# Decay tables by running products in two layouts, first-chunk scores from raw r*k, one rotation for raw weights, and a new order of work

## The chip, the cores and the metric

The kernel runs on 1 core of one Trainium2 chip. The metric is the device time of the whole kernel in microseconds (us). A change of 0.2% of the time before is 1.74 us.

## The reference

Three layers in a row, all in fp32. B = 4 batches, H = 8 heads, S = 768 steps, D = 48; 3072 tokens, d_model 384, d_ff 2048.

```
for t in range(S):                                   # attention with a decaying state
    cur = einsum('bhd,bhe->bhde', u * k[t], v[t])
    y[t] = einsum('bhd,bhde->bhe', r[t], state + cur)
    state = w * state + einsum('bhd,bhe->bhde', k[t], v[t])
x = y as (3072, 384)
h = x @ w_in;  x = (maximum(h, 0) + alpha * minimum(h, 0)) @ w_out      # FF1
h = x @ w_in2; out = (h * tanh(softplus(h))) @ w_out2                    # FF2
```

w (8 x 48) lies between 0.85 and 0.95.

## The kernel before

**Attention by chunks.** A chunk is 128 steps. Inside it the loop becomes matrices: r is multiplied by powers of w that rise with t and k by powers that fall (table RK, by `prep_rk`, L374), and `scores` (L451) multiplies the two on TensorE for all pairs of steps. `masked` (L455, VectorE) copies the strict triangle of the scores into a tile A whose diagonal was preset with c = sum of r*u*k (`preset_first`, L432 on GpSimd or L430 on ScalarE). For the first chunk c comes from `c_first`: a product m of r and k (L389, VectorE), times uw by 8 small matmuls (L393), copied by ScalarE (L395). Since m is made of tiles that `prep_rk` has already scaled by w to the powers t and -(t+1), uw is u*w. `attend0` (L466) multiplies A by v, and `x_first` (ScalarE L160) and `x_first_lo` (VectorE L163) split the result into a high and a low part, fp32r each. The first chunk is units 0 to 3, one per batch. `states_first` (L532) makes the state after it, and ScalarE copies it into T (L534).

Later chunks are units 4 to 23, half a chunk of two batches each. Their heads lie in another layout, the "seats", and `prep_pair` (L380, VectorE) scales r and k by the middle of RKs, the table RK in that layout. Four transfers, SBUF to SBUF, make RKs from RK (`load_RKs`, L271), and `tables_seat` (GpSimd) takes the decay of a half chunk, w64, from it.

**Tables.** `tables` (L308 to L325) makes powers of w by doubling in 24 or so small VectorE instructions, and RK by two multiplies of 112x512.

**FF1.** A slot is 128 of the 2048 features for 512 tokens (units 0 to 3 are one such block): `mA_h` (9 matmuls of 128x512, L238: high x high, high x low, low x high for three pieces of d_model), `mA_g` (ScalarE relu L605, VectorE L607, gives g), `mA_hi` (ScalarE L160), `mA_lo` (VectorE L163), `mA_out` (9 matmuls, L637). In `mA_h` the first matmul needs the high parts of x and of the weight, the second the low part of x, the third the low part of the weight.

**Weights.** Each of the 16 slices of FF1's weights comes raw by one transfer of 768 KB (`more_raw`, `load_raw`, L180), is scaled in two ScalarE passes (`w_scale`, L186 and L187), put together on VectorE (`w_join`, L192) and split (`w_hi` L160 or GpSimd, `w_lo` L163). Slices 0 to 3 land in the places of the later weights w4 to w7, slices 7 to 10 in w9, w11, w13, w15, all others in three buffers "wraw" in rotation: a load there waits for the join of the slice that held the buffer.

**Order.** All work is written out in a plan and sorted by a number per step: the table PLACES gives it by the step's name (a step without an entry has a default), and entries that begin with "?" move a step to another engine. Each engine runs its instructions in that order. `keep_warm` steps (L590) are filler matmuls on a tile of zeros: 8 at the front and 10 in the plan.

Of the kernel before, what the change touches and what calls it, by code (L numbers as in the profile page):

```python
# [54 lines left out]
def more_state(u):  # L55
# [5 lines left out]
    "dma_start": -133.1356, "load_unit 0": -123.5208, "dma_start#": -121.3588, "load_unit 1": -120.2047,  # L61
    "tables": -119.5105, "load_k 0": -116.8818, "load_unit 2": -116.4952, "load_k 2": -116.4633,
    "keep_warm 3########": -115.8159, "dma_start##": -115.6181, "prep_rk 0": -115.3668, "more_raw 1": -115.0907,
    "load_k 1": -114.4474, "load_unit 3": -114.0374, "more_raw 3": -113.632, "pad_v 1": -113.2894,
    "load_unit 4": -111.9708, "more_raw 2": -111.7638, "load_k 3": -111.37, "<lambda> 0": -109.0738,
    "load_unit 5": -107.6626, "tables_u": -106.0724, "<lambda> 1": -105.5347, "memset": -105.2417,
    "keep_warm 3######": -105.0553, "c_first 0": -104.9975, "tensor_scalar": -104.9222, "load_RKs": -104.605,
    "pad_v 0": -103.892, "<lambda> 2": -103.757, "prep_rk 1": -103.5598, "preset_first 0": -103.0121,
    "<lambda> 3": -102.9784, "more_raw 7": -102.3381, "keep_warm 3###": -101.6704, "prep_rk 2": -101.4031,
    "w_scale (0,0)": -101.3169, "keep_warm 3": -101.1634, "keep_warm 3#########": -100.8119, "scale_Kn": -100.7696,  # L70
# [982 lines left out]
```

## Time and profile before

| | |
|---|---|
| median of 3 runs | 872.24 us (871.73 to 872.92) |
| profiled execution, its own time | 871.41 us |
| its span | 869.7 us |
| TensorE (PE) busy, share of the span | 861.4 us, 99% |
| PE weight loads (PEld) | 712.4 us, 82% |
| VectorE (DVE) | 630.6 us, 73% |
| ScalarE (ACT) | 617.5 us, 71% |
| GpSimd (POOL) | 98.9 us, 11% |
| granted TensorE clock | 1.00 |

PE's busy time includes fillers. A share over the whole span says little about the first 51 us, where attention's head, the first weights and the first slots run together; there the rows must be read one by one.

### The profile page before, as it was taken

What the parts mean: (1) busy time and instruction counts of PE and PEld (TensorE: products, weight loads), DVE (VectorE), ACT (ScalarE), POOL (GpSimd) and SP (SyncE); (2) the same over time, 40 slices, a digit from 0 to 9 for tenths busy, and PEclk for the clock granted to TensorE, in tenths of its full rate; (3) what the DMA queues carried; (4) which work ended last, traced back from release to release, by engine and by line L of the source; (5) the groups of instructions that cost most, each with busy time, mean ns of one, the idle gap of its engine ahead of it and who ended that gap; (6) DMA issues with size and microseconds to landing.
All of it is one profiled execution on the core that took longest, in us unless ns stands there. A gap on an engine that the chain in (4) does not pass through costs nothing.

```text
span 869.7 us, 16740 instructions
## 1 busy us (share of the span) xinstructions
PE 861.4 (99%) x6380; PEld 712.4 (82%) x6380; DVE 630.6 (73%) x1021; ACT 617.5 (71%) x1198; POOL 98.9 (11%) x119
## 2 busy tenths in 40 slices
PE   9899999999999999999999999999999999999998
PEld 5778878888888888888888888888888888888897
DVE  6789756657656565554666887887887887887876
ACT  3787765454445545444555998998998998998886
POOL 3624322111122111100002000000000000000000
PEclk9999999999999999999999999999999999999999
DMA  9986365255344426211620200110110110100101
GB/s 316 273 230 208 108 190 146 78 176 152 135 134 141 141 87 212 73 56 64 211 82 35 109 1 1 26 48 1 26 48 1 26 49 0 26 12 1 26 12 37
DMA packets 65840, 80.41 MB, mean 92 GB/s; under 512 B 39712, under 2 KB 52960, under 8 KB 65760
## 3 DMA queue, kind: packets, MB, share of 16 engines
q1 hardware_dynamic: 65200, 79.24, 30.4%
q8 instruction: 50, 0.82, 0.4%
q14 instruction: 30, 0.25, 0.1%
q10 hardware_dynamic: 560, 0.10, 0.1%
HBM read 61.16 MB, written 15.73 MB: 88 GB/s over the span
## 4 chain that ended last, share of the span: by engine, by line
PE 97%; ACT 2%; DVE 1%; issue 0%; POOL 0%; DVEq 0%; POOLq 0%
PE h L238 44%; PE acc L637 22%; PE sc L758 8%; PE acc L758 8%; PE yt L758 4%; PE acc L756 3%; PE acc L590 2%; PE sc L451 2%; PE sc L756 1%; PE h L482 1%; PE yt L503 1%; PE sc L496 1%; PE yt L482 1%; ACT Ah L422 1%; PE h L466 0%
## 5 line engine op out<-in xcount | busy, mean ns | idle before, releaser
L238 PE MATMUL h<-x,w 128*128 128x512 f32 x1728 | 415.8, 390 | 2.8 <-ACT w L160 1.6
L238 PEld LDWEIGHTS h<-x,w 128*128 128x128 f32 x1728 | 323.8, 188 | 72.3 <-ACT w L160 2.0
L637 PE MATMUL acc<-ghi,w 128*128 128x512 f32 x516 | 174.9, 394 | 0.0
L605 ACT ACTIVATE m<-h 128x512 f32<-128x512 f32 x96 | 57.2, 596 | 89.7 <-PE h L238 89.6
L637 PEld LDWEIGHTS acc<-ghi,w 128*128 128x128 f32 x516 | 96.8, 188 | 21.3
L607 DVE SCALAR_TENSOR_TENSOR g<-m,oma,h 128x512 f32<-128x512 f32 x96 | 71.6, 746 | 56.9 <-ACT m L605 55.9
L160 ACT ACTIVATE ghi<-g 128x512 fp32r<-128x512 f32 x86 | 54.1, 629 | 70.9 <-PE acc L637 42.7
L163 DVE TENSOR_TENSOR glo<-g,ghi 128x512 fp32r<-128x512 f32 x86 | 60.3, 701 | 56.3 <-ACT ghi L160 56.1
L637 PE MATMUL acc<-glo,w 128*128 128x512 f32 x258 | 100.4, 389 | 0.0
L695 DVE SCALAR_TENSOR_TENSOR a<-ghi,h 128x512 f32<-128x512 f32 x96 | 66.1, 688 | 37.8 <-ACT ghi L692 31.3
L695 DVE SCALAR_TENSOR_TENSOR g<-s,c 128x512 f32<-128x512 f32 x95 | 66.7, 702 | 22.7 <-ACT s L692 20.6
L703 ACT ACTIVATE m<-h 128x512 f32<-128x512 f32 x96 | 56.4, 588 | 35.0 <-PE h L238 35.0
L163 DVE TENSOR_TENSOR gloB<-g,ghiB 128x512 fp32r<-128x512 f32 x105 | 72.1, 686 | 6.8 <-ACT ghiB L160 6.8
L692 ACT ACTIVATE ghi<-m,biases 128x512 f32<-128x512 f32 x96 | 69.6, 725 | 3.2
L160 ACT ACTIVATE ghiB<-g 128x512 fp32r<-128x512 f32 x105 | 64.8, 617 | 8.8 <-PE acc L637 6.9
L692 ACT ACTIVATE glo<-ghi,biases 128x512 f32<-128x512 f32 x96 | 68.1, 710 | 0.1
L692 ACT ACTIVATE s<-glo,biases 128x512 f32<-128x512 f32 x96 | 68.1, 709 | 0.0
L692 ACT ACTIVATE s<-s,biases 128x512 f32<-128x512 f32 x96 | 68.0, 708 | 0.0
L758 PE MATMUL sc<-ghiB,w 128*128 128x512 f32 x192 | 66.9, 389 | 0.0
L695 DVE SCALAR_TENSOR_TENSOR b<-ghi,a 128x512 f32<-128x512 f32 x96 | 65.7, 684 | 0.1
L695 DVE SCALAR_TENSOR_TENSOR c<-glo,b 128x512 f32<-128x512 f32 x95 | 65.7, 692 | 0.0
L758 PE MATMUL acc<-ghiB,w 128*128 128x512 f32 x192 | 61.7, 389 | 0.0
(198 smaller groups left out, 1157.7 us busy)
## 6 DMA issues: line engine op xcount, KB each, us to landing
wrawr<-in_w SPq DMA_DIRECT2D x24, 768.0 KB, 5.2
nat<-in_nat SPq DMA_DIRECT2D x40, 288.0 KB, 4.3
w2d<-wj SPq DMA_DIRECT2D x16, 384.0 KB, 2.6
wraw<-w2d SPq DMA_DIRECT2D x16, 384.0 KB, 3.0
rk<-in_rkT SPq DMA_DIRECT2D x40, 128.0 KB, 3.0
x2d<-xo SPq DMA_DIRECT2D x6, 768.0 KB, 3.5
x<-x2d SPq DMA_DIRECT2D x6, 768.0 KB, 4.6
rk<-in_rkT SPq DMA_DIRECT2D x40, 96.0 KB, 2.8
```

The costliest lines, as they stand in the source:

```text
L160: act.activation(out=hi, in_=src, func=AF.Copy)
L163: eng.tensor_tensor(out=lo, in0=src, in1=hi.bitcast(F32), op=ALU.subtract)
L238: pe.matmul(h, w_in(layer, f, a, c), x[:, b, c, :], start=(k == 0), stop=(k == 3 * KC - 1))
L451: pe.matmul(sc_t[u][h][HALF[i], o], rk[ROWS[h], 1, j, s], rk[ROWS[h], 0, j, t], start=True, stop=True)
L605: act.activation(out=m, in_=hA[s], func=AF.Relu, scale=-1.0)
L607: dve.scalar_tensor_tensor(out=g, in0=m, scalar=oma[:, f:f + 1], in1=hA.pop(s), op0=ALU.mult, op1=ALU.add)
L637: pe.matmul(acc[0][c], w_out(0, f, a)[:, c * 128:(c + 1) * 128], g[b], start=(f == 0 and k == 0), stop=(f == NF - 1 and k == 2))
L692: act.activation(out=out, in_=in_, func=AF.Square, scale=scale, bias=fin[bias])
L695: dve.scalar_tensor_tensor(out=out, in0=in0, scalar=scalar, in1=in1, op0=op0, op1=ALU.mult)
L703: act.activation(out=bnew("t", n), in_=v["h", n], func=AF.Tanh, scale=0.5)
L756: pe.matmul(acc[1][t][:, :DM], g[a][:, t * C:(t + 1) * C], w_out(1, f, b), **se)
L758: pe.matmul(acc[1][t], w_out(1, f, a)[:, t * 128:(t + 1) * 128], g[b], **se)
```

## The change

- `tables` makes the powers by running products (`tensor_tensor_scan` on VectorE, 68 and 20 elements), one reciprocal of 88 elements, and fills RK by four multiplies of 112x256.
- The seats' table RKs (half as long now, 64 steps) is no longer copied by transfers. Four small transfers on ScalarE's queue bring w in the seats' layout (`wts`), `powers_seat` repeats the running products on VectorE, and `tables_seat` fills RKs by four multiplies of 112x128 on GpSimd ("?seat": 1) and copies w64.
- `m_first` takes the product of raw r and k, ahead of `prep_rk`; the small matmuls then use u itself (`ut`), and `tables_u` goes. The products lie in the buffers glo, glo, ghi and g, where all four shared g.
- Slices 7 to 10 of the raw weights lose their own places and go through the three wraw buffers.
- PLACES is rewritten as a whole. Step switches: presets of the diagonal on ScalarE for unit 3 (before: 2), decay of T on ScalarE for units 4, 6, 8 (before: 8), the sum of unit 7 on ScalarE (before: 9, 10), low parts of the weights 2, 4, 13 on GpSimd (before: 2, 13, 14), fillers 5 and 7 in small pieces (before: 5).

```diff
 PLACES = {
-    "dma_start": -133.1356, "load_unit 0": -123.5208, ...
+    "tables": -134.74003, "powers_seat": -134.4197, "dma_start": -128.3432, "load_unit 0": -125.2362, ...
...
     wt = att.tile([PR, NPR], F32, name="wt")
     w64 = att.tile([PR, NPR], F32, name="w64")
-    uw = att.tile([PR, NPR, 2], F32, name="uw")
-    w96 = att.tile([PR, 40], F32, name="w96")[:, 0:NPR]
+    ut = att.tile([PR, NPR, 2], F32, name="ut")
+    small = att.tile([PR, 40], F32, name="w96")
+    w96, wts = small[:, 0:NPR], small[:, 8:8 + NPR]
...
+    def rows(x):
+        return x.rearrange("d (p n) -> d p n", p=NPR)
+
+    def powers(part, w):
+
+        n, m = NPR * 17, NPR * 5
+        step, first, power, inverse = (part[:, o:o + n + m] for o in (0, 96, 192, 288))
+        P, A = rows(power[:, 0:n]), rows(power[:, n:])
+        iP, iA = rows(inverse[:, 0:n])[:, :, 1:17], rows(inverse[:, n:])
+
+        def scan(at):
+            dve.tensor_tensor_scan(out=power[:, at], data0=step[:, at], data1=first[:, at], initial=0.0, op0=ALU.mult,
+                                   op1=ALU.add)
+
+        pool.memset(part, 0.0)
+        for x in (rows(first[:, 0:n]), rows(first[:, n:])):
+            pool.memset(x[:, :, 0], 1.0)
+        dve.tensor_copy(rows(step[:, 0:n])[:, :, 1:17], w.unsqueeze(2).to_broadcast([PR, NPR, 16]))
+        scan(slice(0, n))
+        dve.tensor_copy(rows(step[:, n:])[:, :, 1:5], P[:, :, 16:17].to_broadcast([PR, NPR, 4]))
+        scan(slice(n, n + m))
+        dve.reciprocal(out=inverse, in_=power)
+        return ((P[:, :, 0:16], iA, A), (iP, A, iA))
+
+    def fill(eng, table, parts, n):
+
+        for i, (p, less, more) in enumerate(parts):
+            o = table[:, i].rearrange("d p (a b) -> d p a b", b=16)
+            for a, g in ((0, less[:, :, n:0:-1]), (n, more[:, :, 0:n])):
+                eng.tensor_tensor(out=o[:, :, a:a + n], in0=g.unsqueeze(3).to_broadcast([PR, NPR, n, 16]),
+                                  in1=p.unsqueeze(2).to_broadcast([PR, NPR, n, 16]), op=ALU.mult)
+
     def tables():
 
-        part = new("g")[0:PR].rearrange("d (p x) -> d p x", p=NPR)
-        P, iP, G, iG = part[:, :, 0:17], part[:, :, 32:48], part[:, :, 64:73], part[:, :, 80:89]
-        sq = part[:, :, 96:98].transpose([0, 2, 1])
-
...
+        fill(dve, RK, parts, 4)
+        A = parts[0][2]
+        dve.tensor_tensor(out=w96, in0=A[:, :, 4], in1=A[:, :, 2], op=ALU.mult)
+
+    seat_t = {}
+
+    def powers_seat():
+        seat_t[0] = powers(per.tile([128, 512], F32, tag="w0", name="seat")[0:PR], wts)
 
     def tables_seat():
 
-        pool.tensor_tensor(out=w64, in0=RKs[:, 1, :, 0], in1=RKs[:, 0, :, HC + 1], op=ALU.mult)
-
-    def load_RKs():
-        by_seat(RKs, RK, slice(None))
+        fill(pool if other("seat") else dve, RKs, seat_t[0], 2)
...
-    w_stage = {0: "w4", 1: "w5", 2: "w6", 3: "w7", 7: "w9", 8: "w11", 9: "w13", 10: "w15"}
+    w_stage = {0: "w4", 1: "w5", 2: "w6", 3: "w7"}
...
-        w = RKs.rearrange("d i p t -> d (i p) t")[:, :, HC // 2:HC // 2 + HC]
+        w = RKs.rearrange("d i p t -> d (i p) t")
...
+    m_t = {}
+
+    def m_first(u):
+        rk = inp[u][0]
+        m_t[u] = (new("g") if u == 3 else new(("glo", "glo", "ghi")[u], bufs=2))[0:PR].rearrange("d (p s) -> d p s", p=NPR)
+        (pool if other(f"m {u}") else dve).tensor_tensor(out=m_t[u], in0=rk[:, 0], in1=rk[:, 1], op=ALU.mult)
+
     def c_first(u):
 
-        rk = inp[u][0]
-        m = new("g")[0:PR].rearrange("d (p s) -> d p s", p=NPR)
-        (pool if other(f"m {u}") else dve).tensor_tensor(out=m, in0=rk[:, 0], in1=rk[:, 1], op=ALU.mult)
+        m = m_t[u]
         y = yt_t[u] = bank(*(("yt",), ("acc1",), ("h", 2), ("h", 2))[u])
         t = y[:, KC * C:KC * C + H]
         for p in range(NPR):
-            pe.matmul(t[:, 2 * p:2 * p + 2], m[:, p, :], uw[:, p, :], start=True, stop=True)
...
         pool.memset(w96, 0.0)
         for q in range(2):
-            act.dma_start(out=uw[ROWS[q], :, q], in_=ub[0].rearrange("(p q d) -> q d p", p=NPR, q=2)[q])
+            act.dma_start(out=ut[ROWS[q], :, q], in_=ub[0].rearrange("(p q d) -> q d p", p=NPR, q=2)[q])
+        by_seat(act, wts, wT)
...
-        at(-102.9, load_RKs)
         at(-102.8, more_raw, 3)
         at(-102.7, load_unit, B + 1)
         at(-102.6, more_raw, 7)
         for u in range(B):
             at(-103.35 + 0.001 * u, lambda u: pool.memset(vz_t[u][:, :, :, 0:D], 0.0), u)
         at(-103.34, pool.memset, T, 0.0)
-        at(-100.4, tables_seat)
+        at(-103.315, powers_seat)
+        at(-103.314, tables_seat)
         at(-103.32, tables)
-        at(-103.31, tables_u)
         at(-100.5, tensor_scalar)
         at(-101, scale_Kn)
         for i in range(2):
...
+            at(E["rk"][u] - 0.001, m_first, u)
```

What the new PLACES do is shown by the instructions of three engines at one place of the program, around the first two slots of FF1 (`mA_h 0` and `mA_h 1`).

TensorE before, from the attention of unit 3 on (A_381 is unit 3's tile, acc2_466 the state of units 0 and 1, acc0 a filler, h_490 and h_504 the first two slots):

```order
L466 MATMUL h_336<-A_381,w15u_162 64x128 x6
L466 MATMUL h_336<-A_381,w15u_162 48x128 x6
L532 MATMUL acc2_466<-w9u_121 48x48 x8
L532 MATMUL acc2_466<-w11u_126 48x48 x8
L590 MATMUL acc0_487<-ghi_96 128x384
L238 MATMUL h_490<-x_384,w0_345 128x512 x9
L238 MATMUL h_504<-x_384,w1_485 128x512 x9
```

TensorE of the change, the same piece (acc2_427 is the state, A_349 unit 3's tile, h_498 and h_536 the first two slots):

```order
L676 MATMUL acc2_427<-w9u_148 48x48 x8
L676 MATMUL acc2_427<-w11u_156 48x48 x8
L734 MATMUL acc0_447<-ghi_96 128x384
L734 MATMUL acc0_458<-ghi_96 128x384
L610 MATMUL h_289<-A_349,w15u_164 64x128 x6
L610 MATMUL h_289<-A_349,w15u_164 48x128 x6
L734 MATMUL acc0_494<-ghi_96 128x128 x3
L367 MATMUL h_498<-x_325,w0_390 128x512 x9
L367 MATMUL h_536<-x_325,w1_394 128x512 x9
```

The state now comes ahead of two fillers and of unit 3's attention.

ScalarE before, from the high part of x of unit 3 (h_336) on (w6r and w7r are the raw slices 2 and 3, Ah the diagonal of unit 4, T the state, w1 and w2 the high parts of slices 1 and 2):

```order
L160 ACTIVATE x_384<-h_336 128x3x128
L186 ACTIVATE w6r_167<-w6r_167 128x768
L187 ACTIVATE w6r_167<-w6r_167 128x768
L422 ACTIVATE Ah_457<-cst_94,cc_402 128x64 x8
L534 ACTIVATE T_100<-acc2_466 48x8x48 x2
L160 ACTIVATE w1_485<-wj_375 128x768
L186 ACTIVATE w7r_213<-w7r_213 128x768
L187 ACTIVATE w7r_213<-w7r_213 128x768
L160 ACTIVATE w2_547<-wj_502 128x768
```

ScalarE of the change (h_255, acc1_244 and h_289 are units 2, 1 and 3):

```order
L289 ACTIVATE w1_394<-wj_392 128x768
L289 ACTIVATE x_325<-h_255 128x3x128
L678 ACTIVATE T_100<-acc2_427 48x8x48 x2
L289 ACTIVATE x_325<-acc1_244 128x3x128
L315 ACTIVATE w6r_185<-w6r_185 128x768
L316 ACTIVATE w6r_185<-w6r_185 128x768
L289 ACTIVATE x_325<-h_289 128x3x128
L566 ACTIVATE Ah_486<-cst_94,cc_460 128x64 x8
L315 ACTIVATE w7r_336<-w7r_336 128x768
L316 ACTIVATE w7r_336<-w7r_336 128x768
L749 ACTIVATE m_532<-h_498 128x512
L289 ACTIVATE w2_565<-wj_466 128x768
```

The high part of slice 1 (w1) moved ahead of the copies of T, and the diagonal of unit 4 (Ah) behind all parts of x.

VectorE before, from the low part of x of unit 2 (h_267) on (acc1_236, h_336 and yt_195 are units 1, 3 and 0; nat_180 the sum of unit 4, rk_170 and rk_171 its r and k, wj the joined slices):

```order
L163 TENSOR_TENSOR x_384<-h_267,x_384 128x3x128
L163 TENSOR_TENSOR x_384<-acc1_236,x_384 128x3x128
L410 TENSOR_REDUCE cc_402<-nat_180 128x8
L163 TENSOR_TENSOR x_384<-h_336,x_384 128x3x128
L163 TENSOR_TENSOR x_384<-yt_195,x_384 128x3x128
L380 TENSOR_TENSOR rk_170<-rk_170,RKs_98 112x1024
L163 TENSOR_TENSOR w1_485<-wj_375,w1_485 128x768
L192 SCALAR_TENSOR_TENSOR wj_502<-w6r_167 128x768
```

VectorE of the change (h_255, yt_170, h_289 and acc1_244 are units 2, 0, 3 and 1; the first scaling of unit 4, rk_198, stands ahead of this piece, between the two mask copies of unit 3):

```order
L292 TENSOR_TENSOR x_325<-h_255,x_325 128x3x128
L321 SCALAR_TENSOR_TENSOR wj_466<-w6r_185 128x768
L554 TENSOR_REDUCE cc_460<-nat_208 128x8
L292 TENSOR_TENSOR x_325<-yt_170,x_325 128x3x128
L292 TENSOR_TENSOR x_325<-h_289,x_325 128x3x128
L292 TENSOR_TENSOR x_325<-acc1_244,x_325 128x3x128
L292 TENSOR_TENSOR w1_394<-wj_392,w1_394 128x768
```

The join of slice 2 (wj_466) and the sum of unit 4 now stand ahead of three of the four low parts of x, and the low part of slice 1 right behind them.

## Rows read from the trace of the kernel before

**Rows 1.** Table by stretch: length; busy PE, PEld, DVE, ACT, POOL; clock; DMA; GB/s.

```profile
0.00:32.20 32.20, 30.61 (x347) 22.06 (x348) 22.44 (x42) 13.02 (x33) 14.75 (x23) 1.00 0.91 280
32.20:50.80 18.60, 15.81 (x240) 11.63 (x238) 15.21 (x22) 17.27 (x38) 8.79 (x10) 1.00 0.91 282
50.80:115.00 64.20, 64.20 (x758) 53.08 (x759) 51.61 (x88) 48.26 (x115) 24.82 (x24) 1.00 0.65 186
```

**Rows 2.** The page's costliest groups: busy and mean ns; idle before, releaser.

```profile
L238 PE MATMUL h<-x,w 128*128 128x512 f32 x1728 | 415.8, 390 | 2.8 <-ACT w L160 1.6
```

**Rows 3.** Timeline of PE from 32 us: start, duration, group, idle before and releaser.

```profile
32.24 0.69 PE L238 MATMUL h<-x,w 128*128 128x512 f32 x1
33.21 2.11 PE L238 MATMUL h<-x,w 128*128 128x512 f32 x8 [0.28 <-DVE x L163]
36.95 0.73 PE L238 MATMUL h<-x,w 128*128 128x512 f32 x2 [1.63 <-ACT w L160]
37.94 1.89 PE L238 MATMUL h<-x,w 128*128 128x512 f32 x7 [0.26 <-DVE w L163]
...
50.75 4.37 PE L238 MATMUL h<-x,w 128*128 128x512 f32 x18 [0.50 <-DVE g L607]
```

**Rows 4.** Timeline of PE ahead of 32 us.

```profile
10.49 0.95 PE L393 MATMUL yt<-uw,g 112*128 112x2 f32 x8
...
22.08 0.94 PE L590 MATMUL acc<-ghi 128*128 128x128 f32 x6
...
29.56 1.58 PE L466 MATMUL h<-A,w15u 128*64 128x128 f32 x24
30.87 0.53 PE L532 MATMUL acc<-w9u 128*48 128x48 f32 x14
...
31.79 0.91 PE L590 MATMUL acc<-ghi 128*128 128x384 f32 x2
```

**Rows 5.** Timeline of ACT around the first slot.

```profile
31.18 0.49 ACT L160 ACTIVATE x<-h 128x384 fp32r<-128x384 f32 x1 [0.46 <-PE h L466]
31.57 0.90 ACT L186 ACTIVATE w6r<-w6r 128x768 f32<-128x768 f32 x1
...
35.06 0.97 ACT L534 ACTIVATE T<-acc 48x384 f32<-48x384 f32 x2
```

**Rows 6.** Timeline of DVE around the first slot.

```profile
24.99 1.36 DVE L455 COPY_PREDICATED A<-cst,sc 128x512 f32<-128x512 uint32 x2 [0.75 <-PE sc L451]
...
31.68 0.55 DVE L410 TENSOR_REDUCE cc<-nat 128x8 f32<-128x384 f32 x1
...
32.61 0.55 DVE L163 TENSOR_TENSOR x<-yt,x 128x384 fp32r<-128x384 f32 x1
34.71 1.48 DVE L380 TENSOR_TENSOR rk<-rk,RKs 112x1024 f32<-112x1024 f32 x1 [1.55 <-DMA RKs<-RK]
...
37.80 0.95 DVE L192 SCALAR_TENSOR_TENSOR wj<-w6r 128x768 uint32<-128x768 uint32 x1
```

**Rows 7.** Timeline of DVE and POOL in the head.

```profile
5.66 1.22 DVE L308 TENSOR_TENSOR RK<-g 112x512 f32<-112x512 f32 x2
...
11.74 1.32 POOL L432 TENSOR_SCALAR_AFFINE_SELECT A<-cc 128x1024 f32<-128x1024 f32 x1 [8.70 <-ACT cc L395]
12.02 1.58 DVE L389 TENSOR_TENSOR g<-w10u 112x512 f32<-112x512 f32 x1
...
15.93 0.69 DVE L389 TENSOR_TENSOR g<-w12u 112x512 f32<-112x512 f32 x1 [2.33 <-PE acc L393]
...
21.20 1.00 POOL L414 TENSOR_TENSOR w9u<-w9u,Kn 128x384 f32<-128x384 f32 x1
```

**Rows 8.** Timeline of ACT's DMA issues.

```profile
0.97 0.88 ACTq L881 DMA_DIRECT2D uw<-in_ub  x2
```

**Rows 9.** Transfers: KB each, median us from issue to landing.

```profile
w13r<-in_w SPq DMA_DIRECT2D x1, 768.0 KB, 11.9
...
RKs<-RK SPq DMA_DIRECT2D x2, 128.0 KB, 7.3
...
uw<-in_ub ACTq DMA_DIRECT2D x2, 0.8 KB, 2.1
```

More of the change, by code (lines that the diff above doesn't have):

```diff
@@ L60 @@
 PLACES = {
[L61 to L70, printed above, removed]
[10 rows of a table removed]
@@ L81 @@
-    "table_Kn 1": -94.0098, "half_tables": -93.6758, "x_first 2": -93.4186, "x_first_lo 2": -93.2056,
[5 rows of a table removed]
-    "prep_c 5": -9.0485, "scores 4": -7.5643, "w_hi (0,2) False": -5.3917, "w_join (0,3)": -4.9708,
[4 rows of a table removed]
-    "states_first 2": 1.8509, "w_lo (0,3)": 1.8993, "batch 4": 1.9228, "tables_seat": 1.9613, "t_decay 4": 1.9898,
[3 rows of a table removed]
-    "mA_hi 2": 3.1417, "t_update 4": 3.2014, "w_hi (0,5) True": 3.2114, "mA_out 1": 3.2317, "mA_lo 2": 3.2509,
[3 rows of a table removed]
-    "mA_out 2": 4.5282, "w_join (0,6)": 4.6373, "mA_hi 4": 4.6446, "mA_lo 4": 4.9016, "w_hi (0,6) False": 4.963,
@@ L123 @@
-    "w_lo (0,13)": 12.7923, "mA_hi 12": 12.8951, "mA_out 11": 13.2099, "mA_h 13": 13.2418, "w_scale (0,15)": 13.3173,
-    "w_lo (0,14)": 13.4463, "w_join (0,15)": 13.4797, "w_hi (0,15) True": 13.6321, "mA_h 14": 13.7794,
[8 rows of a table removed]
+    "tables": -134.74003, "powers_seat": -134.4197, "dma_start": -128.3432, "load_unit 0": -125.2362,
+    "load_unit 2": -123.4258, "load_unit 1": -123.0306, "<lambda> 2": -122.9803, "load_k 2": -122.4801,
+    "m_first 0": -121.8326, "load_unit 3": -121.8174, "keep_warm 3####": -121.53864, "prep_rk 0": -121.0596,
@@ new lines @@
+    "c_first 0": -117.65627, "dma_start#": -117.2357, "<lambda> 1": -116.85421, "pad_v 0": -115.89302,
+    "pad_v 1": -115.81874, "more_raw 3": -115.7731, "w_scale (0,0)": -115.49469, "more_raw 2": -115.3498,
+    "dma_start##": -115.1339, "load_k 1": -113.3095, "scale_Kn": -111.77466, "load_k 0": -110.91822,
+    "keep_warm 3": -110.2728, "memset": -110.23645, "<lambda> 0": -110.0655, "load_unit 4": -105.99025,
[11 rows of a table added]
+    "w_hi (0,0) False": -96.3571, "w_join (0,1)": -96.05688, "w_hi (0,1) False": -96.04175, "prep_kn 0": -95.72893,
@@ new lines @@
+    "scores 3": -95.2575, "masked 3 0": -95.25578, "attend0 2": -95.2513, "x_first 2": -95.24333,
+    "states_first 0": -94.7865, "x_first 1": -94.6942, "keep_warm 3#": -94.69168, "tables_seat": -94.6882,
[9 rows of a table added]
+    "mA_lo 0": -1.26398, "load_unit 7": -0.9527, "?warm 5": 1, "?warm 7": 1, "?preset 3": 1, "?seat": 1, "?hi 3": 1,
+    "?lo 2": 1, "?decay 4": 1, "?lo 4": 1, "?hi 7": 1, "?sum 7": 1, "?decay 6": 1, "?pair 8 0": 1, "?lo 13": 1,
+    "?hi 15": 1, "?decay 8": 1, "w_scale (0,4)": 1.49608, "mA_g 1": 1.6875, "w_hi (0,3) True": 1.70452,
@@ new lines @@
+    "states_first 2": 1.8509, "batch 4": 1.87525, "w_lo (0,3)": 2.1103, "mA_hi 1": 2.2917, "mA_lo 1": 2.3517,
+    "w_scale (0,5)": 2.37587, "t_decay 4": 2.4193, "w_join (0,4)": 2.43649, "w_hi (0,4) False": 2.4398,
[8 rows of a table added]
+    "mA_g 5": 4.9113, "batch 5": 4.9611, "w_hi (0,7) True": 5.0767, "w_hi (0,6) False": 5.1766,
[4 rows of a table added]
+    "w_join (0,9)": 6.8343, "w_hi (0,9) True": 6.85157, "mA_hi 6": 6.85437, "mA_lo 6": 6.8665,
[4 rows of a table added]
+    "w_hi (0,10) False": 8.5586, "x_parts 6": 8.6069, "mA_h 9": 9.00701, "mA_hi 8": 9.1133, "w_scale (0,11)": 9.15983,
@@ new lines @@
+    "mA_out 7": 9.2125, "w_lo (0,10)": 9.24428, "mA_h 10": 9.25715, "w_join (0,11)": 9.2593, "t_decay 6": 9.329,
+    "mA_lo 8": 9.4802, "more_raw 15": 9.6915, "prep_pair 8 0": 9.7741, "preset 7 1": 9.80857, "mA_g 9": 9.93347,
+    "mA_hi 9": 9.95468, "w_hi (0,11) True": 10.02223, "w_lo (0,11)": 10.0529, "prep_c 8": 10.1685,
+    "prep_kn 8": 10.17246, "mA_out 8": 10.19297, "t_update 6": 10.2012, "masked 7 1": 10.298,
+    "w_scale (0,12)": 10.3047, "mA_lo 9": 10.4426, "mA_h 11": 10.5628, "mA_g 10": 10.6056, "w_join (0,12)": 10.7625,
@@ L133 @@
+    "mA_hi 10": 10.7992, "mA_lo 10": 10.8653, "w_hi (0,12) False": 10.8802, "mA_g 11": 10.89, "mA_hi 11": 11.04234,
[3 rows of a table added]
+    "mA_g 12": 12.1844, "w_hi (0,14) False": 12.45664, "mA_hi 12": 12.46381, "batch 7": 12.4901,
[137 rows of a table added]
 }
@@ L264, in half_tables, with by_seat @@
             pool.tensor_copy(id2[h], cst[h, i * HC:(i + 1) * HC])
-    def by_seat(out, in_, *lead):
+    def by_seat(queue, out, in_, *lead):
         for q, h, rows in ((0, 0, (0, 64, 0)), (1, 1, (48, 112, 48)), (0, 1, (0, 48, 64)), (1, 0, (64, 112, 0))):
             a, b, o = rows
-            dma.dma_start(out=out[(slice(o, o + b - a),) + lead + (slice(2 * q, 2 * q + 2),)],
+            queue.dma_start(out=out[(slice(o, o + b - a),) + lead + (slice(2 * q, 2 * q + 2),)],
                           in_=in_[(slice(a, b),) + lead + (slice(2 * h, 2 * h + 2),)])
@@ L290, in load_unit @@
             for i in range(2):
-                by_seat(rk_t[j, bp][i], rkT[B * j + 2 * bp + i], slice(None))
+                by_seat(dma, rk_t[j, bp][i], rkT[B * j + 2 * bp + i], slice(None))
         n = att.tile([128, 3, DM], F32, tag="nat", name="nat", bufs=3)
@@ L297, in attention_and_two_ff @@
     RK = per.tile([PR, 2, NPR, C], F32, tag="w1", name="RK")
-    RKs = att.tile([PR, 2, NPR, C], F32, name="RKs")
+    RKs = att.tile([PR, 2, NPR, HC], F32, name="RKs")
     Kn = att.tile([128, 2, NPR, 2, D], F32, name="Kn")
     T = att.tile([PR, B, NPR, 64], F32, name="T")
-    def tables():
-        part = new("g")[0:PR].rearrange("d (p x) -> d p x", p=NPR)
-        P, iP, G, iG = part[:, :, 0:17], part[:, :, 32:48], part[:, :, 64:73], part[:, :, 80:89]
-        sq = part[:, :, 96:98].transpose([0, 2, 1])
-        def mul(o, x, y):
-            dve.tensor_tensor(out=o, in0=x, in1=y, op=ALU.mult)
-        def wide(x, n):
-            return x.unsqueeze(2).to_broadcast([PR, NPR, n])
-        pool.memset(P[:, :, 0], 1.0)
-        dve.tensor_copy(P[:, :, 1], wt)
-        for n in (1, 2, 4, 8):
-            mul(P[:, :, n + 1:2 * n + 1], P[:, :, 1:n + 1], wide(P[:, :, n], n))
-        w16 = P[:, :, 16]
-        mul(sq[:, 0], w16, w16)
-        mul(sq[:, 1], sq[:, 0], sq[:, 0])
-        dve.reciprocal(out=G[:, :, 0], in_=sq[:, 1])
-        for n, w in ((1, w16), (2, sq[:, 0]), (4, sq[:, 1])):
-            mul(G[:, :, n:2 * n], G[:, :, 0:n], wide(w, n))
-        mul(G[:, :, 8], G[:, :, 7], w16)
-        dve.reciprocal(out=iP, in_=P[:, :, 1:17])
-        dve.reciprocal(out=iG, in_=G)
-        for i, (g, p) in enumerate(((G, P[:, :, 0:16]), (iG, iP))):
-            mul(RK[:, i].rearrange("d p (a b) -> d p a b", b=16), g[:, :, 0:8].unsqueeze(3).to_broadcast([PR, NPR, 8, 16]),
-                p.unsqueeze(2).to_broadcast([PR, NPR, 8, 16]))
-        mul(w96, sq[:, 1], sq[:, 0])
@@ L331, in tables_u @@
-    def tables_u():
-        dve.tensor_tensor(out=uw, in0=uw, in1=wt.unsqueeze(2).to_broadcast([PR, NPR, 2]), op=ALU.mult)
+    def rows(x):
[17 more added lines that the diff above has]
+        return ((P[:, :, 0:16], iA, A), (iP, A, iA))
@@ new lines, in fill @@
+    def fill(eng, table, parts, n):
[4 more added lines that the diff above has]
+                                  in1=p.unsqueeze(2).to_broadcast([PR, NPR, n, 16]), op=ALU.mult)
+    def tables():
+        parts = powers(new("g")[0:PR], wt)
+        fill(dve, RK, parts, 4)
+        A = parts[0][2]
+        dve.tensor_tensor(out=w96, in0=A[:, :, 4], in1=A[:, :, 2], op=ALU.mult)
@@ L334, in tables_seat @@
+    seat_t = {}
+    def powers_seat():
+        seat_t[0] = powers(per.tile([128, 512], F32, tag="w0", name="seat")[0:PR], wts)
     def tables_seat():
-        pool.tensor_tensor(out=w64, in0=RKs[:, 1, :, 0], in1=RKs[:, 0, :, HC + 1], op=ALU.mult)
-    def load_RKs():
-        by_seat(RKs, RK, slice(None))
+        fill(pool if other("seat") else dve, RKs, seat_t[0], 2)
+        pool.tensor_copy(w64, seat_t[0][0][2][:, :, 4])
     kw_t = {}
@@ L392, in c_first @@
         for p in range(NPR):
-            pe.matmul(t[:, 2 * p:2 * p + 2], m[:, p, :], uw[:, p, :], start=True, stop=True)
+            pe.matmul(t[:, 2 * p:2 * p + 2], m[:, p, :], ut[:, p, :], start=True, stop=True)
         c_t[u] = None, new_c(u)
```

7 lines of the change are left out of this document (1 added, 6 removed), and 226 rows, old and new, of the table PLACES.

## The prediction

> **What bounds the kernel now.** I read the page first: TensorE is busy for 99% of the span, so time can only be won where TensorE waits or works without need. The table by stretch says where that is. From 50.80 us TensorE is busy for 64.20 of 64.20 us [rows 1], and the later slots go on like this; whatever the new order does there cannot be gained, only lost. From 32.20 to 50.80 us it is busy for 15.81 of 18.60 us: 2.8 us lie idle. In the first 32.20 us it is busy for 30.61, but part of that is fillers. A matmul's record is longer than its share of the stream: the mean is 390 ns [rows 2], while 18 in a row last 4.37 us [rows 3], which is (4.37 - 0.39) / 17 = 0.234 us a step. So behind an idle time of x the loss is x + 0.39 - 0.23, about x + 0.16.
>
> The timeline of TensorE then names the waits [rows 3]: the second matmul of the first slot waits for the low part of x (33.21, idle 0.28), the second slot for the high part of weight 1, from ScalarE (36.95, idle 1.63), then for its low part (37.94, 0.26), and a later slot for g of VectorE, which must have read a bank of h before it is filled again (50.75, 0.50). The first two slots, 18 matmuls, end at 37.94 + 7 x 0.234 = 39.58 us.
>
> **The head, to the first slot.** TensorE has the same matmuls and the same 18 fillers before and after, in another order, and in before it waits nowhere for long there (30.61 of 32.20 [rows 1]). Whatever becomes ready sooner, TensorE cannot reach the first slot much before 32.24 [rows 3]. One thing is worse: scores of unit 3 now stand close behind those of unit 2 in the same banks and must wait for two mask copies, 1.36 us [rows 6], with one filler of 0.91 [rows 4] between: 0.45, say 0.5. The first slot starts at 32.7.
>
> **The first two slots: minus 0.6.** The state of units 0 and 1 now comes ahead of two fillers, unit 3's attention and a split filler. Going back from 32.7 by 0.77 (22.08 to what follows a split filler, of records of 0.94 that overlap), 1.31 (29.56 to 30.87) and twice 0.84 (fillers of 0.91 that overlap) [rows 4], the state is done at 28.9. ScalarE's chain behind it: T's copies 0.97, x of unit 1 0.49, two passes over weight 2 at 0.90 [rows 5], to about 32.2. VectorE's join of weight 2 stands ahead of three low parts of x and needs those passes: 0.95 [rows 6], to 33.1; then the sum and three low parts, four instructions of 0.47 each (31.68 to 32.61 is two) [rows 6], to 35.0. So a new wait appears: the second matmul of the first slot starts at 35.0, not 33.21. But weight 1 is no longer late: its high part stands ahead of all this on ScalarE, and its low part ends at 35.0 + 0.96, ahead of the second slot's third matmul (35.0 + 10 x 0.234 = 37.3). The 17 matmuls that are left end at 35.0 + 17 x 0.234 = 38.98, against 39.58. With the passes 1 us later or earlier this term runs from +0.4 to -1.6; where VectorE is not late at all it is 32.7 + 18 x 0.234 = 36.9, or -2.7.
>
> **The wait for g: minus 0.66.** In before g came late because a weight's high part and the diagonal of unit 5 stood ahead of its relu on ScalarE. After, that diagonal stands behind the relu and behind two high parts. I walk slots 2 to 5 with the durations of before and find g 1.5 to 2 us ahead of its need. The wait costs 0.50 + 0.16 = 0.66 [rows 3]; bounds 0 and 0.66.
>
> **Edits priced at nothing.**
> - Tables: RK by two multiplies took 1.22 us at 5.66 [rows 7]; four of half the size cost the same or a little more, and the small instructions become five. No scan is in the trace; I bound one between nothing and 0.61, the multiply of 112x512 [rows 7], and take 0.2. The raw product comes sooner than before as well. All of it is hidden by the fillers ahead of the first small matmuls, at 10.49 [rows 4]; without them the gain would be about 1 us. The Trainium skill ("DVE: opcode table, instruction layouts, handler registers and perf-mode slots", section 6) says that the scan runs at half throughput; no run so far shows it.
> - The seats' table without its transfers: VectorE waited 1.55 us for them, but at 34.71 [rows 6], where TensorE waited for ScalarE. This is the sort of gain that does not reach the time.
> - Its cost is on GpSimd: four fills of 128 elements. 384 elements take 1.00 [rows 7], so one is between 0.33 and 1.00; I take 0.6, nearer to the smaller count, 2.4 in all. They start at about 24 us: the diagonal of unit 2 (1.32) uses unit 0's tile and waits for its attention, done by my walk at 20.7, and two multiplies (1.00) follow; they end at 26.5. Behind them wait, on VectorE, the scaling of unit 4 and, queued behind that, the second mask copy of unit 3, which unit 3's attention needs by 30.6. The slack is 1 to 2 us: hidden, and at 1.00 each still within 0.7.
> - One shared port speaks against it. At 12.02 a VectorE multiply took 1.58 us beside a GpSimd instruction that ran from 11.74 for 1.32, and 0.69 alone at 15.93 [rows 7]. It ended at 13.60; if it waited for the other's end at 13.06, 0.54 is left for its own work. The Trainium skill ("SBUF — State Buffer", Who interferes with whom) has it that a VectorE instruction with two SBUF inputs and a GpSimd one that reads SBUF lock each other out for a whole instruction; this row agrees. By it each fill may cost VectorE its own 0.6; the sum leaves that to the slack.
> - Seats' w: six instead of two issues on ScalarE's queue at 0.44 each (0.88 for two at 0.97 [rows 8]) end at 3.6; landing 2.1 later as for uw [rows 9], at 5.7.
>
> **Sum.** -0.6 - 0.66 = -1.3 us. The profiled execution took 871.41 (span 869.7), so it would take 870.1; it lies 0.83 under the median of 872.24, and for the median I forecast 870.9.
>
> **Rivals.**
> - *Nothing is late on VectorE.* If masks, fills and passes run a little faster than I walk them, the new wait for x shrinks to nothing: -2.7 - 0.66 = -3.4, 868.9. For it: ScalarE and VectorE are busy for 17.27 and 15.21 of 18.60 us there [rows 1], so half a microsecond early goes through the whole chain. Against: three instructions of others' work stand in the chain by the written order.
> - *The waits only move.* VectorE reaches the low parts of x 0.6 later, and another g is late for 0.66: 0, 872.2. For it: the same two busy engines; every new position displaces another.
> - *Raw weights late (the other sign).* Slice 7 has lost its own place and waits for the join of slice 4, done at about 45.3; queued behind its ScalarE passes is the high part of g of slot 3, whose `mA_out` I find due at 57.2. Landing takes 11.9 for the slowest of the old slices 7 to 10 [rows 9]: 45.3 + 11.9 = 57.2, then passes 1.7, high part 0.6, low part 0.7: 3.0 late. With issue 0.7 later, as SP's queue has eight slow transfers ahead, 3.7: 872.24 - 1.3 + 3.7 = 874.6. The time gets longer than before once it lands after 55.5 (57.2 - 3.0 + 1.3). Against: the loads now come one by one, and not three at once.
> - *Tables late, the change does not do what it says.* VectorE makes the seats' running products ahead of the first raw product. If their w takes 7.3 us to land, as the transfers of RKs did [rows 9], and not 2.1, it is there at 10.9; with products of 1.6 and 0.69 the first small matmuls start at 13.2, not 10.49 [rows 4]: +2.7 - 1.3, 873.6. It decides from a landing at 8.2 on.
>
> A measurement of this kernel can tell about 0.2%, 1.74 us, from no change: faster is below 870.50, slower above 873.98.
>
> **How the numbers follow.** Forecast 46% (its own range 870.0 to 872.0; 16 of the 46 below 870.50), nothing late 25%, waits only move 13%, raw weights late 11%, tables late 5%. Faster: 16 + 25 = 0.41. Slower: 11 and, of tables late, 4 = 0.15. Same: the rest, 0.44. The range leaves out 11 at the top (raw weights), and the far ends of nothing late and of tables late, some 9: from 868.5 to 873.3.
>
> **What the profile after would show.** The first FF1 matmul at 32.5 to 32.9; its second waiting for VectorE's low part of x until about 35.0; no wait for weight 1; the first two slots done by 39.0; no wait for g up to 55 us; no transfer ahead of the first scaling of unit 4; GpSimd's fills done by 27; then TensorE without gaps. The prediction is wrong if TensorE reaches the first slot much before 32.2 or past 33, if the second matmul waits past 36, or if a gap opens between 50 and 60 us behind raw slice 7.

## The result

The change makes the kernel slower: a median of 882.0 us in 6 runs (880.22 to 885.16) against 872.33 (871.73 to 872.92, 6 runs), a ratio of 1.0105 with a 95% interval of 1.0088 to 1.0122. The forecast was 870.9, and its range ended at 873.3. The profiled execution took 885.16 us, its span is 883.4; it is the longest of the six, so what the clock costs in it is the upper end.

The page of the profile after shows TensorE as busy as before, 10.9 us longer. The first line of part 2 is TensorE's busy share by fortieths of the span, the second its granted clock: in the first two fortieths, some 44 us, it is 0.7.

```profile
PE 872.3 (99%) x6384; PEld 718.5 (81%) x6384; DVE 635.7 (72%) x1017; ACT 618.0 (70%) x1190; POOL 106.3 (12%) x128
PE   8989999999999999999999999999999999999998
PEclk7799999999999999999999999999999999999999
```

The table by stretch, made finer for the change (columns as in [rows 1]), says when the clock fell. From about 5 us on it is granted in full (2.4 GHz), at half (1.2 GHz) from 11.5 to 32 us, and in full from then on. Before, it is 1.00 over all of that [rows 1]. In the first 4.7 us (before: 5.3) the trace has no record of the clock, and the view shows 1.00 for want of one: the fillers run at a step of 0.64 us there and of 0.32 afterwards, as the counts of TensorE's matmuls in the first two lines show (4 and 8).

```profile
2.00:4.00 2.00, 2.00 (x4) 1.00 (x3) 1.22 (x4) 0.00 (x0) 1.04 (x5) 1.00 0.88 140
6.00:8.00 2.00, 2.00 (x8) 1.10 (x6) 1.05 (x3) 0.00 (x0) 1.58 (x2) 1.00 1.05 308
8.00:10.00 2.00, 1.29 (x4) 0.30 (x2) 1.73 (x5) 0.00 (x0) 0.91 (x3) 1.00 0.79 290
10.00:12.00 2.00, 0.79 (x5) 0.79 (x5) 1.97 (x3) 0.00 (x0) 0.00 (x0) 0.87 1.00 382
12.00:14.00 2.00, 2.00 (x7) 1.20 (x6) 2.00 (x4) 0.52 (x3) 0.85 (x1) 0.50 1.07 421
...
30.00:32.00 2.00, 2.00 (x24) 1.98 (x22) 0.00 (x0) 0.00 (x0) 0.28 (x1) 0.51 1.03 390
32.00:34.00 2.00, 2.00 (x30) 1.74 (x28) 0.00 (x0) 1.35 (x5) 2.00 (x3) 1.00 1.04 433
```

The timeline of TensorE in the change shows what went ahead of it, and where the time went.

```profile
1.31 8.04 PE L734 MATMUL acc<-ghi 128*128 128x384 f32 x18 [1.31 <-POOL ghi L1028]
11.21 1.65 PE L537 MATMUL yt<-ut,glo 112*128 112x2 f32 x8 [1.86 <-DVE glo L529]
...
44.64 0.48 PE L367 MATMUL h<-x,w 128*128 128x512 f32 x1
47.22 4.15 PE L367 MATMUL h<-x,w 128*128 128x512 f32 x17 [2.11 <-DVE x L292]
...
66.41 1.89 PE L367 MATMUL h<-x,w 128*128 128x512 f32 x7 [0.72 <-DVE w L292]
```

TensorE is through its fillers at 9.35 and idles 1.86 us for the first raw product. The eight small matmuls then take 1.65 us and not 0.95 [rows 4]: most of that runs at half clock. The first FF1 matmul comes at 44.64, 12.4 us after that of before (32.24 [rows 3]). So 1.86 us are the gap itself, and nearly all of the rest, some 10.5, is what twenty microseconds at half clock lose. Behind it the wait for the low part of x is there as forecast (2.11).

VectorE's and GpSimd's timelines show why the product was late.

```profile
6.18 0.16 DVE L468 TENSOR_TENSOR w<-g 112x4 f32<-112x4 f32 x1
7.30 1.66 DVE L448 COPY seat<-w 112x64 f32<-112x64 f32 x1 [0.95 <-DMA w<-in_wT]
9.06 0.30 DVE L442 TENSOR_TENSOR_SCAN seat<-seat 112x68 f32<-112x68 f32 x1
9.39 0.17 DVE L450 COPY seat<-seat 112x16 f32<-112x16 f32 x1
9.67 0.20 DVE L442 TENSOR_TENSOR_SCAN seat<-seat 112x20 f32<-112x20 f32 x1
9.91 0.70 DVE L452 RECIPROCAL seat<-seat 112x88 f32<-112x88 f32 x1
10.53 0.63 DVE L529 TENSOR_TENSOR glo<-w8u 112x512 f32<-112x512 f32 x1
```

```profile
6.42 1.04 POOL L485 TENSOR_TENSOR m<-RK,w 112x512 f32<-112x512 f32 x1 [3.32 <-DVE w L468]
7.40 0.95 POOL L974 MEMSET T<- 112x1024 f32 x1
8.29 0.34 POOL L1050 MEMSET w9u<- 128x288 f32 x1
8.57 0.34 POOL L1050 MEMSET w15u<- 128x288 f32 x1
```

The common table is done at 6.3. Then VectorE waits 0.95 us for the seats' w, its first copy takes 1.66 us, to 8.96, just behind the end of GpSimd's last fill (8.91), and the rest of the seats' products follow; only then comes the raw product that TensorE needs. The w itself comes late from ScalarE's queue: four issues, then the time from issue to landing (the last column).

```profile
1.91 2.29 ACTq L401 DMA_DIRECT2D w<-in_wT  x4
w<-in_wT ACTq DMA_DIRECT2D x2, 0.5 KB, 3.7
```

### The profile page after: what moved, and what is told of

Same layout as the page of the kernel before. It is cut to its first block, busy times and chain, and to the rows that moved or that the text cites. A ratio compares the mean times of both kernels' runs of the same rounds, so it can differ in the third digit from the quotient of the medians.

```text
span 883.4 us, 16747 instructions
## 1 busy us (share of the span) xinstructions
PE 872.3 (99%) x6384; PEld 718.5 (81%) x6384; DVE 635.7 (72%) x1017; ACT 618.0 (70%) x1190; POOL 106.3 (12%) x128
## 4 chain that ended last, share of the span: by engine, by line
PE 88%; ACT 3%; DMA 1%; DVE 1%; issue 1%; SPq 1%; DVEq 0%; ACTq 0%; POOL 0%; POOLq 0%
PE h L367 42%; PE acc L781 21%; PE sc L902 7%; PE acc L902 7%; PE yt L902 4%; PE acc L900 3%; PE sc L595 1%; PE sc L900 1%; PE h L626 1%; DMA x<-y 1%; PE yt L647 1%; DMA nat<-in_nat 1%; PE sc L640 1%; ACT wrawr L316 1%; PE yt L626 1%
```

## The experiments

Each is timed beside the kernel before on the same chip. Ratios are to that one, with 95% intervals. It spreads too: beside these runs from 871.23 to 877.66 us, at mean granted clocks of 1.000 to 0.994, so the ratio counts and not the difference from 872.33.

**e1: the seats' products later, first try.**

```diff
-"powers_seat": -134.4197
+"powers_seat": -100.89
```

> The change with one step moved: the seats' running products (five VectorE instructions, 10.53 - 7.30 = 3.2 us with their waits) stand behind the first three raw products, not ahead of them. Theory A (they make the first raw product late, TensorE idles 1.86 us at 9.35, and after that its clock is granted at half until about 32 us): no wait at the first small matmuls, granted clock 1.00 throughout, first FF1 matmul at 32.3 to 33.0 and not 44.64, time 869.5 to 873. Theory B (the new order of the head is slow in itself, or something else lowers the clock): the first FF1 matmul still past 40 us, time 878 to 885.

Measured: 885.15 us, ratio 1.0131 (1.0110 to 1.0153). The first small matmuls started at 9.04 without a wait, but a new one came behind them, a fault of the edit: the step's fills with zeros on GpSimd moved along, behind a diagonal that waits for its sums. VectorE waited for those (5.89 us), TensorE for its masks:

```profile
23.30 1.99 PE L595 MATMUL sc<-w10u 48*64 48x64 f32 x32 [7.56 <-DVE A L599]
```

The clock is 1.00 up to 18 us and then at half until about 31: it fell inside this gap. So the run doesn't test the order of the head; it shows the same fall at another gap.

**e2: the gap filled with work.**

```diff
+        at(-119.0, keep_warm, 2)
```

> The change with two more fillers (0.91 us each at full clock) ahead of the first small matmuls and nothing else: the first raw product stays as late as it is, 10.5 us. Theory A (the idle time of 1.86 us costs little by itself; what costs is the half clock that follows it): TensorE has no gap at 9.35, clock 1.00, first FF1 matmul near 32.7 + 1.8 = 34.5, time 871 to 875, so added work makes the kernel 8 us faster. Theory B (TensorE's own lateness is what counts, or the new order is slow): 880 to 885.

Measured: 876.06, ratio 1.0042 (1.0027 to 1.0057). More work and an equally late product, and 6 us less than the change. No gap ahead of the small matmuls, clock 1.00 in the profile, first FF1 matmul at 35.02; no run has a mean clock under 0.996 (the change: 0.988 to 0.992). It is a little over the range that theory A gave, by losses behind 80 us (below, e6).

```profile
11.31 0.95 PE L537 MATMUL yt<-ut,glo 112*128 112x2 f32 x8
10.00:12.00 2.00, 2.00 (x11) 1.40 (x12) 1.97 (x3) 0.00 (x0) 0.00 (x0) 1.00 0.82 303
```

**e3: the kernel before, with the product made late.**

```diff
         mul(w96, sq[:, 1], sq[:, 0])
+        for _ in range(3):
+            mul(RKs, RK, RK)
```

> The kernel before with three multiplies of 112x1024 added on VectorE at the end of the tables (3 x 1.2 us), into a tile that is overwritten later: the only thing that this adds is 3.5 us of lateness for the first product, so that TensorE idles about 1.9 us at 10.5. Theory A: the granted clock falls to half after it, as in the change, and the time is 878 to 885. Theory B (a gap alone does not lower the clock; the change's other order or its matmuls do): the gap shows, the clock stays at 1.00, and the time is 872 to 875.

Measured: 876.35, ratio 1.0030 (1.0015 to 1.0046), between the two theories. The wait and the fall of the clock are there (0.63 and 0.76 in the two stretches), yet the clock is back at 1.00 by 20 us, not at 32. It falls once more for 3.4 us at 42, behind the waits of the first two slots. Two of the ten runs have a mean clock of 1.00, at 873.8, so the fall does not come in every run.

```profile
12.56 1.05 PE L395 MATMUL yt<-uw,g 112*128 112x2 f32 x8 [2.42 <-DVE g L391]
```

```profile
12.00:14.00 2.00, 1.44 (x10) 1.19 (x10) 2.00 (x3) 0.35 (x3) 0.09 (x1) 1.00 1.01 406
14.00:16.00 2.00, 1.93 (x4) 0.42 (x2) 2.00 (x2) 1.73 (x3) 2.00 (x3) 0.63 1.04 421
16.00:20.00 4.00, 3.89 (x32) 2.47 (x36) 0.69 (x2) 0.43 (x3) 1.33 (x3) 0.76 1.04 361
20.00:24.00 4.00, 4.00 (x70) 3.02 (x60) 3.58 (x5) 1.60 (x6) 1.91 (x2) 1.00 0.79 173
```

A gap lowers the clock in the old order too, but what it costs differs: 3.6 us at the first FF1 matmul here, 12.4 in the change.

**e4: GpSimd's fills with zeros out of the way.**

```diff
-"memset": -110.23645, "<lambda> 0": -110.0655, "<lambda> 3": -104.45837
+"memset": -104.09, "<lambda> 0": -104.08, "<lambda> 3": -104.07
```

> The change with three GpSimd fills with zeros (T, and the v tiles of units 0 and 3; 0.95 and twice 0.34 us) moved behind the first diagonal, so that they no longer run beside the first copy of the seats' products, which took 1.66 us instead of the 0.61 of its twin in the tables. If VectorE's copy waits for GpSimd, it takes 0.5 to 0.8 us here and the first small matmuls start at 10.1 to 10.4, with a gap of about 0.9 us and not 1.86. If the shorter gap does not lower the clock, the time is 871 to 874; if it does, 878 to 884. If the copy is long for another reason, nothing changes.

Measured: 876.18, ratio 1.0047 (1.0029 to 1.0065). The copy takes 0.74 us, so it did wait for GpSimd. What is left goes with GpSimd's multiply, which ends at 7.46, the copy at 7.51; alone the same copy takes 0.18 (e5, e11).

```profile
6.77 0.74 DVE L448 COPY seat<-w 112x64 f32<-112x64 f32 x1 [0.43 <-DMA w<-in_wT]
9.08 0.63 DVE L529 TENSOR_TENSOR glo<-w8u 112x512 f32<-112x512 f32 x1
```

The ten runs spread from 873.56 (mean clock 0.999) to 881.76 (0.992). The profiled one is the shortest: in it the fillers' step fell from 0.64 to 0.32 us only at 7.3 us (the change: 4.7), so that TensorE came to the small matmuls late itself, without a gap.

**e5 to e8: without the late product, what is left?** e5 keeps the fills at the front (`clear_seat`, split off) and moves the five VectorE instructions behind the scaling of unit 3. The other three build on it.

```diff
-"powers_seat": -134.4197
+"clear_seat": -134.4197, "powers_seat": -98.0
 # e6 = e5 and
-tag="y3", name="y3", bufs=1
+tag="y3", name="y3", bufs=2
 # e7 = e5 and
-w_stage = {0: "w4", 1: "w5", 2: "w6", 3: "w7"}
+w_stage = {0: "w4", 1: "w5", 2: "w6", 3: "w7", 7: "w9", 8: "w11", 9: "w13", 10: "w15"}
 # e8 = e6 and, on VectorE, "w_join (0,2)" and "prep_c2 4" behind "x_first_lo 1"
```

> The seats' running products again moved, now without the fault of e1: their GpSimd fills with zeros stay at the front, and the five VectorE instructions stand behind the scaling of unit 3's r and k. In e1 the fills had moved too and stood on GpSimd behind a diagonal that waits for its sums, so VectorE, the masks and TensorE (7.56 us) waited. Theory A (products in front of the first raw product, then the half clock): no gap before the first FF1 matmul above 0.4 us, clock 1.00, first FF1 matmul at 32.3 to 33.0, time 871 to 873.5: most of the change's 9 to 10 us are gone in every run. Theory B (the head's new order itself): first FF1 matmul past 36, time above 877.

> e5 with two buffers in place of one for y3, the tile through which the fourth pair of heads of later units goes by transfers. In the trace of e4 (full clock) ScalarE stood 3.16 us at 76.5 for these transfers of unit 5 before it could write y3 of unit 6, and the slots from 81 to 107 us lost some 2.6 us in small waits for weights and g. Theory C (that wait is the cause of the later losses): ScalarE does not wait there, time 2 to 3 us below e5. Theory D (the raw weights' rotation through three buffers makes them late): time within 0.7 us of e5.

> e5 with the raw slices 7 to 10 in places of their own, as before. Theory C (y3's transfers are the cause of the losses from 81 to 107 us): within 0.7 us of e5, unless the transfers of y3 come sooner for it. Theory D (raw slices late in the rotation): 2 to 3 us below e5.

> e6 with the join of weight 2 and the sum of unit 4 behind the low parts of x on VectorE. In e4 the second matmul of the first slot waited 1.70 us for these low parts. If the order of VectorE is the cause, the wait falls to 0.3 us or less and the time by 1.0 to 1.5 us against e6; if weight 2 or g then comes late by as much, it is within 0.5 us of e6.

Measured: e5 876.5 (ratio 1.0029, 1.0013 to 1.0045), e6 874.08 (1.0007, 0.9991 to 1.0023), e7 875.34 (1.0014, 0.9994 to 1.0034), e8 876.63 (1.0025, 1.0006 to 1.0045).

*e5* has no gap above 0.29 us ahead of the first FF1 matmul, and 5.5 us of the loss are gone. But in half of its 12 runs the mean clock is 0.994, and in its profile it is at half from 16 to 26 us, with no gap ahead of that. Theory A had said 1.00: here the clock falls without a gap.

*e6 and e7* settle the loss behind 80 us. How much later than in before a slot starts grows from slot 8 to the end by 1.05 us in e5, 1.25 in e7 and 0.05 in e6. ScalarE's wait for y3's transfers is 1.59, 1.78 and none:

```profile
83.69 0.22 ACT L289 ACTIVATE y<-yt 112x64 fp32r<-112x64 f32 x1 [1.59 <-DMA x<-y]
```

```profile
80.87 0.23 ACT L289 ACTIVATE y<-yt 112x64 fp32r<-112x64 f32 x1 [0.59 <-PE h L656]
```

The first line is e5's, the second e6's. So theory C holds and the raw weights' rotation costs nothing that shows. In the change itself this wait is 3.15 us, and the same difference 2.6 us.

*e8* removes most of the wait for x (0.56 us left), and it comes back at once as a wait for g and one for unit 4's masks. From the first slot to the third e8 takes 1.4 us more than e6: the waits only move, as that rival of the prediction has it.

```profile
39.23 4.35 PE L367 MATMUL h<-x,w 128*128 128x512 f32 x17 [0.56 <-DVE x L292]
45.82 0.27 PE L635 MATMUL h<-rk,T 48*64 48x64 f32 x1 [0.76 <-DVE g L760]
47.38 0.69 PE L604 MATMUL sc<-rk 48*64 48x64 f32 x32 [1.10 <-DVE Ah L608]
```

**e9, e10: is it the row of narrow matmuls?**

```diff
 # e9 = e6 and
-"keep_warm 3##": -100.90567, "keep_warm 3########": -100.2836
+"keep_warm 3##": -104.9, "keep_warm 3########": -101.0
 # e10 = the kernel before and
-"keep_warm 3#": -99.6762, "keep_warm 3##": -98.3856
+"keep_warm 3#": -100.51, "keep_warm 3##": -100.505
```

> e6 with the same fillers, two of them moved: one between the scores of unit 0 and the table's transposes, one between the sums of units 1 and 2, where e5 and e6 have 3.2 us of narrow matmuls (scores 0, transposes, two sums, 11.1 to 14.3 in e6) in a row and both fillers behind them. In e5, e6 and e8 the clock fell to half at 15.3 to 16.5 though TensorE had no gap; in before, where fillers stand between those steps, it stayed at 1.00 in the profiled run. Theory E (the row of narrow matmuls lowers the clock as a gap does): clock 1.00 in the profile, a mean clock of 0.998 or more in at least 9 of 12 runs (e6: 8 of 12), median 871 to 872.5, 1.5 to 3 us below e6. Theory F (chance, or something else in the new head): as e6, 873.5 to 875.

> The kernel before with two fillers moved ahead of the sum of unit 1, so that this sum, the scores of unit 0, the sum of unit 2, the transposes and the scores of unit 1 stand in a row without fillers, some 4.7 us of narrow matmuls; the work is the same. Theory E (such a row lowers the clock): the clock falls to half within some us behind the row in most runs, time 874 to 878. Theory F: within 0.2% of before, clock as before.

Measured: e9 874.1 (ratio 1.0004, 0.9990 to 1.0019), e10 873.21 (0.9997, 0.9982 to 1.0011). With the fillers spread no run of e9 has a mean clock under 0.997 (e6: 4 of 12 at 0.994), but bunching them in the kernel before changes neither its time nor the clock of the head, which is 1.00 up to 38 us in the profile (it falls there, behind a wait of 1.59 us for weight 1). A long row without fillers is thus not enough; why the clock falls in e5 to e8, each without a gap, stays open. e9's time gains nothing, against theory E: a wait of 1.91 us for unit 1's masks appears, behind the seats' products, whose scan took 1.16 us beside a diagonal on GpSimd:

```profile
23.47 0.43 PE L619 MATMUL acc<-A,w11u 128*64 128x128 f32 x2 [1.91 <-DVE A L608]
18.05 1.09 POOL L585 TENSOR_SCALAR_AFFINE_SELECT A<-cc 128x1024 f32<-128x1024 f32 x1 [5.82 <-ACT cc L548]
...
18.13 1.16 DVE L448 TENSOR_TENSOR_SCAN seat<-seat 112x68 f32<-112x68 f32 x1
```

**e11: all waits of the head moved out; e12: the change with e9's fillers alone.**

```diff
 # e11 = e9 and
-"powers_seat": -98.0
+"powers_seat": -121.0, "memset": -104.09, "<lambda> 0": -104.08, "<lambda> 3": -104.07, "w_scale (0,0)": -100.92
 # e12 = the change and
-"keep_warm 3##": -100.90567, "keep_warm 3########": -100.2836
+"keep_warm 3##": -104.9, "keep_warm 3########": -101.0
```

> e9 with three more steps moved, each out of a wait that the traces show: the seats' running products into VectorE's wait for r and k of unit 1 (2.6 us idle at 8.9 to 11.5 in e7), GpSimd's fills with zeros of T and two v tiles behind the first diagonal (in e4 this took the products' first copy from 1.66 to 0.74 us), and the passes over weight 0 on ScalarE behind the sums of units 1 and 2 (in e9 these stood 4.09 us behind a transfer of weight 0, and the diagonals with them). If the head's waits were what is left of the loss: no gap above 0.4 us ahead of the first FF1 matmul, which starts at 32.3 to 33.2, and a median of 870 to 872, faster than before by 0.2% or even with it. If new waits take their place: 873 or more.

> The change with the two fillers of e9 moved between the narrow matmuls, and nothing else: the seats' products still stand first, so that the gap of 1.5 to 1.9 us ahead of the first small matmuls stays. Theory G (the gap lowers the clock, and the row of narrow matmuls behind it keeps it low for 20 us): the half clock lasts under 8 us, 875 to 878. Theory H (the gap alone makes the whole loss): the half clock lasts some 15 to 20 us, 880 to 885, as in the change.

Measured: e11 871.87 (870.65 to 872.57, 12 runs), ratio 0.9985 (0.9974 to 0.9996), faster than before by 0.15%, less than the 0.2% that count as a change. Its timeline has a clean head, and then the forecast's own wait:

```profile
9.72 0.95 PE L546 MATMUL yt<-ut,glo 112*128 112x2 f32 x8
...
33.05 0.48 PE L367 MATMUL h<-x,w 128*128 128x512 f32 x1
35.68 5.73 PE L367 MATMUL h<-x,w 128*128 128x512 f32 x17 [2.15 <-DVE x L292]
```

Here the clock fell behind that wait (17 matmuls last 5.73 us, not 4.15). In the runs at a mean clock of 1.00 the time is 870.65 to 872.33.

e12 is at 883.37, ratio 1.0087 (1.0053 to 1.0122): theory H, the gap makes the loss, fillers between the narrow matmuls behind it do not help. In its profile the gap is there and the clock at half from 11.5 to 32 us, as in the change:

```profile
10.93 1.39 PE L537 MATMUL yt<-ut,glo 112*128 112x2 f32 x8 [1.58 <-DVE glo L529]
```

Its runs, time and mean granted clock, show that one program can come out at either end:

```
873.8 0.999   876.3 0.997   877.2 0.996   882.5 0.990   884.3 to 885.1 0.988 (four runs)
```

## Why the prediction was wrong, by its steps

- **The step that failed** is "All of it is hidden by the fillers ahead of the first small matmuls, at 10.49", with its companion on the seats' w. Three sizes in it were off. TensorE is there at 9.35, not 10.49: nine fillers stand ahead of the small matmuls and not ten, and in this execution they reached their shorter step 0.7 us sooner than in before (at 4.7 and 5.3). The seats' w is there at 7.3, not 5.7: four issues took 2.29 us and the landing 3.3 to 3.7, not 2.1 as for uw [rows 9]. And the seats' products took 3.2 us, not 1.6: the copy waited for GpSimd, and dependent instructions of 0.2 to 0.7 us left up to 0.11 us between them. The product came at 11.16. The granted clock stands in no term of the sum: it was put at nothing without a reason.
- **The rival was there, its price was not.** "Tables late" named this mechanism and gave it +2.7 and 5%. It asked for a landing from 8.2 us on; the w was there by 7.3, and the product was late even so. It counted a late microsecond as a microsecond. The gap was shorter than that, 1.86, and cost 12.4 with the half clock behind it. (Nor does it follow that 4 of its 5% are counted as slower: its 873.6 lies below the 873.98 at which slower begins.) Covering the gap with fillers (e2), bringing the product sooner (e4), or taking its cause away (e5, e11) each took some 5 to 10 us off; making it alone (e12) kept the loss, and a like gap in the kernel before (e3) lowered its clock as well.
- **The first two slots** were near. In the change, from the first matmul of slot 0 to the last of slot 1, 6.35 us pass against 7.20 in before: 0.85 won, where the forecast has 1.1 (0.6, and the 0.5 by which it starts them later). e11 has the first FF1 matmul at 33.05 (said: 32.7), and its second 2.63 us later (said: 2.3); weight 1 is not waited for. Against before, e6 takes 0.61 us less from the start of slot 0 to that of slot 1, and 1.35 less from there to slot 2: weight 1's low part, and 0.7 in the row of unit 4's matmuls, which I had not counted.
- **The wait for g** is gone, as said: slot 3 gains another 0.66 in e6. In the change 0.72 us come in its place at 66.41, for weight 5's low part, which is in no term. That instruction took 1.76 us on VectorE behind a GpSimd multiply that had started 0.07 us ahead of it; in e6 the two start together, and it is GpSimd that takes longer (the first two lines are the change's, the others e6's):

```profile
64.52 1.02 POOL L546 TENSOR_TENSOR nat<-nat 128x384 f32<-128x384 f32 x1
64.59 1.76 DVE L292 TENSOR_TENSOR w<-wj,w 128x768 fp32r<-128x768 f32 x1
57.53 1.85 POOL L555 TENSOR_TENSOR nat<-nat 128x384 f32<-128x384 f32 x1
57.54 0.95 DVE L292 TENSOR_TENSOR w<-wj,w 128x768 fp32r<-128x768 f32 x1
```

- **y3's transfers** are in no step of mine: the new order brings unit 6's copies forward, onto a buffer whose transfers are still under way. Price 2.6 us in the change. Read at the starts of the slots, the 13.7 us by which the profiled span is longer are 12.4 ahead of the first FF1 matmul, 2.3 won over slots 0 to 4, 1.0 lost at weight 5 and 2.6 behind slot 8.
- **Raw weights late** did not happen: e7 against e5.
- Without the gap and y3's wait the sum may have been near, which is not shown for the change as it stands: e11 moves other steps too. Its six runs at a mean clock of 1.00 have a median of 871.5, against the 870.9 that was said, and the median of all twelve is 871.87.

## What to carry to other kernels

An edit that is "hidden by fillers" is hidden only up to the microsecond at which the fillers end: count them again in the new order, and walk to that point everything that now stands ahead of the awaited instruction, its transfer included. Where a gap can be followed by half clock, price it by what the clock does after it, not by its length. And when one program's runs spread by several microseconds, set each time beside its mean clock before explaining a difference.
